# The experts' products taken in the order 0, 7, 1, 6, 2, 5, 3, 4, with one buffer and a share of the pooling moved beside it

## The chip, the core and the metric

One core of a Trainium2 chip runs the whole program in one launch. Its engines are TensorE (PE, with its weight loads listed as PEld), VectorE (DVE), ScalarE (ACT), GpSimd (POOL) and SyncE (SP), which issues most transfers; 16 DMA engines move the data. The metric is the time of one execution on the device in microseconds (us), the median of several runs.

## The reference, cut to what matters

Three layers follow one another: attention (a pooled one plus a local one), a mixture of experts, and a mixing layer over tokens and channels. There are 4 batches of 576 tokens, 512 channels (8 heads of 64), 8 experts with 1024 hidden units, and 1536 hidden channels in the mixing layer.

```python
# attention: q, k, v averaged over 4 tokens for the pooled part; a band of +-3 tokens for the local part
k_d = k.reshape(B, H, Sd, factor, D).mean(axis=3)
out = repeat(sm_attn(q_d, k_d, v_d), 4) + softmax(band(q @ k.T)) @ v
# mixture of experts: one expert a token, chosen in order of the tokens
for s in range(S):
    fresh_e = int(np.argmax(logits[b, s]))
    e = fresh_e if s == 0 or local_gate[b, s] < 0.5 else prev_e
    h = np.maximum(x[b, s] @ w1[e], 0.0)
    out[b, s] = p[e] * (h @ w2[e])
# mixing: the weights are float64, a token product and then a channel product
u = x + (np.maximum(xt @ w_tok1, 0.0) @ w_tok2).transpose(0, 2, 1)
return (u + np.maximum(u @ w_ch1, 0.0) @ w_ch2).astype(np.float32)
```

## The kernel before, in words

The program has three stages, each with its own hand-written scheduler (`Sched`). A stage's code only lists operations; `Sched.order` then gives every engine a fixed order of instructions, from costs written in the source, from the free buffers and from a due time (`stage`) that the code sets while it lists them. The order is fixed before the program runs, so an engine that waits at one instruction also holds up all that stand behind it. Transfers that SP issues are one such queue.

**Attention** (`Attn`) runs over the 4 batches. `pool_k` adds up four keys at a time: either one reduction on VectorE (64x768 to 64x192), or three additions on GpSimd; the table `KDVE` lists the pairs of batch and half that go to VectorE. `pool_v` does the same for the values of the batches 1 to 3, on GpSimd from a ring of buffers `raw` (`NRAW` of them), into which the values are loaded. The ring `vw` (`NVW` buffers of the same size) holds the values of the local attention. `p` is the softmax of the local part: VectorE sums it, GpSimd divides by the sum. `route` numbers the tokens of each expert.

Behind the last batch's products, the two experts with most tokens so far get a first block of 256 rows each (`Early`). Its weights come chunk by chunk into `raw`, and are split into a high and a low part, which lie in the attention's rings `kz` (high) and `vw` (low). Each product of two fp32 matrices is made of three matrix products of such parts.

**The experts** (`Moe`) run by rank, which is the order of the experts by tokens left. Rank r has room for `CAPS[r]` rows: 384, 376, 320, 288, 256, 256, 192 and 128. A rank's weights come in 8 chunks of 512 KB, issued by SP into a ring of 3 buffers (`raw`, tiles `raw_27xx`), then split by ScalarE (`wh`, a cast) and VectorE (`wl`, a difference) into rings of 4 (3, and the pair `l_wh`, `l_wl`). For each chunk, `mm1` makes 128 hidden units of all the rank's rows (12 products with as many columns as rows, at least 256), ScalarE and VectorE make the two parts of the ReLU (`h`), and `mm2` adds them into the output in PSUM (`y`, 4 banks; three products of 512 columns a tile of 128 rows). Rank 7 is an exception: its `mm1` reads the unsplit `raw` buffer (4 products), so that this buffer is free only after `mm1`, and only half a chunk is split. `gather` fetches the rows of the next rank. Filling the spare rows of the output with zeros (`zeros`) takes 8 transfers of 512 KB and some small ones.

Every second chunk from the ninth to the forty-ninth also lists one `convert`, 21 in all: it turns 512 columns of the mixing layer's float64 weights into two fp32 parts. That is a transfer of 512 KB (`cr`), three operations on VectorE (`cf`), a square on ScalarE (`cs`), two operations on GpSimd (`cs`, `cf`), a cast on ScalarE and a difference on VectorE (`wtl`, `c1l`, `c2l`).

**The mixing layer** (`Mix`) then gathers the tokens' rows from memory (`yd`) and runs its products.

Of the kernel before, what the change touches and what calls it, by code (L numbers as in the profile page):

```python
# [21 lines left out]
NE = 8  # L22
# [13 lines left out]
KF = FF // 128  # L36
# [183 lines left out]
class Sched:  # L220
# [80 lines left out]
    def i(self, e, m, after=(), **kw):  # L301
        outs = [kw[k] for k in ("out", "accum_out") if kw.get(k) is not None]
        ins = [v for k, v in kw.items() if k not in ("out", "accum_out") and isinstance(v, (bass.AP, View))]
        acc = [(region(a), True) for a in outs] + [(region(a), False) for a in ins]
        c = self.cost(e, m, outs[0], ins, kw)
        if self.cur is not None:
            o = self.ops[self.cur]
            assert o["e"] == e
            o["calls"].append((m, kw))
            o["d"] += c  # L310
        else:
            self.ops.append(dict(e=e, calls=[(m, kw)], d=c, pred={}, use=[], init=None, stage=self.stage + self.shift, moves=True))
        k = len(self.ops) - 1
        o = self.ops[k]
        for p in after:
            o["pred"].setdefault(p, 0)
        for a in outs + ins:
            if isinstance(a, View) and a.buf not in o["use"]:
                o["use"].append(a.buf)
                a.buf.users.append(k)  # L320
        self.note(k, acc)
        return k
# [211 lines left out]
class Attn:  # L534
# [108 lines left out]
    def pool_k(self, b, pr):  # L643
# [5 lines left out]
        for u in range(2):  # L649
            r = slice(64 * u, 64 * u + 64)  # L650
            kv = kz[r, u, :, 3:195].rearrange("p h (g r) -> p h g r", r=4)
            kd = s["kd"][r, :, 48 * pr:48 * pr + 48]
            if (b, u) in KDVE:
                i("dve", "tensor_reduce", out=kd, in_=kv, axis=AX.X, op=ALU.add)
# [266 lines left out]
    def run(self, early):  # L921
        S_ = self.S
        do = lambda name, b, *args: S_.late((name, b), getattr(self, name), b, *args)
        do("load_q", 0)
        self.load_consts()
        for b in range(B):
            t0 = STEP * 3 * b
            S_.stage = t0 - D_LEAD * STEP if b else D0
            if b:
                do("load_q", b)  # L930
            for pr in range(3):
                do("load_u", b, pr)
                do("pool_k", b, pr)
                if pr:
                    do("pool_v", b, pr - 1)
            for hp in range(HP):
                do("pool_q", b, hp)
                do("d1", b, hp)
                do("d2", b, hp)
            for pr in range(3):  # L940
                S_.stage = t0 + STEP * pr
                do("l1", b, pr)
                do("l2", b, pr)
                for n in ((0,), (1, 2), (3, 4))[pr]:
                    do("x1", b, n)
            S_.stage = t0 + 3 * STEP + R_LAG * STEP
            if b == B - 1:
                stage, S_.stage = S_.stage, t0 + E_LAG * STEP
                S_.late("take", self.early.take)
                S_.stage = stage  # L950
            elif b == B - 2:
                S_.stage = t0 + 3 * STEP + E_LAG * STEP
            do("route", b)
            if b == B - 3:
                self.early = early()
# [142 lines left out]
def convert(S_, src, n, hi, lo, after=(), cf="cf", cs="cs", queue="dma"):  # L1098

    i = S_.i  # L1100
    raw = S_.next("cr")
    if src.dtype == mybir.dt.int64:
        i(queue, "dma_start", after=after, out=raw[:, 0:2 * n], in_=src.bitcast(I32))
        rv = raw[:, 0:2 * n].rearrange("p (n t) -> p n t", t=2)
        low, high = rv[:, :, 0], rv[:, :, 1]
        f = S_.next(cf, I32)[:, 0:n]
        i("dve", "tensor_scalar", out=f, in0=high, scalar1=3, scalar2=0x3FFFFFF8, op0=ALU.logical_shift_left, op1=ALU.bitwise_and)
        i("dve", "scalar_tensor_tensor", out=f, in0=low, scalar=29, in1=f, op0=ALU.logical_shift_right, op1=ALU.bitwise_or)
        i("dve", "scalar_tensor_tensor", out=f, in0=high, scalar=-0x40000000, in1=f, op0=ALU.bitwise_and, op1=ALU.bitwise_or)
        sq = S_.next(cs, F32)[:, 0:n]  # L1110
        i("act", "activation", out=sq, in_=high.bitcast(F32), func=AF.Square)
        f = f.bitcast(F32)
        i("pool", "tensor_single_scalar", out=sq, in_=sq, scalar=FLOOR, op=ALU.is_ge)
        i("pool", "tensor_tensor", out=f, in0=f, in1=sq, op=ALU.mult)
    else:
        f = raw.bitcast(F32)[:, 0:n]
        i(queue, "dma_start", after=after, out=f, in_=src)
    i("act", "copy", out=hi, in_=f)
    i("dve", "tensor_tensor", out=lo, in0=f, in1=hi.bitcast(F32), op=ALU.subtract)
# [249 lines left out]
            self.late("loadw", self.n)  # L1369


class Moe(Experts):
    LO, CUT, QUEUE = "dve", 4, "dma"

# [52 lines left out]
    def run(self):  # L1427
        NW = KF * NE
        prev, done = None, []
        t0 = 0.0  # L1430
        for n in range(NW):
            r, fb = divmod(n, KF)
            self.S.stage = t0
            t0 += 4 * (12 * CAPS[r] / 2400 + TILES[r] * 0.65)
            if n >= NLEAD:
                self.loadw(n)
            if fb == 3 and r + 1 < NE:
                self.gather(r + 1)
            h = self.mm1(r, fb)
            if prev is not None:  # L1440
                self.mm2(*prev)
            prev = (r, fb, h)
            done.append(len(self.S.ops) - 1)
            if n == 24:
                self.S.stage = t0
                self.zeros()
            if n >= 8 and n % CONV == 0 and self.jobs:
                self.S.stage = t0 + 60
                convert(self.S, *self.jobs.pop(0), after=(done[n - 6],))
        self.mm2(*prev)  # L1450
        assert not self.jobs
        self.S.issue(self.S.order(busy=dict(pe=PE_LATE)))
# [264 lines left out]


WARM, WINDOW = 0.5, 3.4
NKZ, NVW, NRAW = 5, 4, 3  # L1720
VPE = (0,)
KDVE = ((0, 0), (0, 1), (1, 0), (2, 0), (3, 0))
STEP, D_LEAD, R_LAG = 12.0, 1.0, 1.5
SLACK = 0.02
PE_LATE = 2.0
# [30 lines left out]
```

## Time and profile before

| what | value |
|---|---|
| median of 3 runs | 818.68 us (816.3 to 821.28) |
| the profiled execution | 815.2 us, of which 813.4 us are the span of the trace |
| PE, DVE, ACT, POOL busy | 764.6, 464.5, 331.1, 231.5 us |
| granted TensorE clock, mean | 0.987 |
| attention and early block | 0 to 214.9 us |
| experts | 214.9 to 438.3 us |
| mixing layer | from 448.0 us |

Engines work side by side, so their busy times don't add up to the span. A busy time says how much of a stretch an engine worked; what a change is worth is read from what the waiting engine waits for. Times in rows are microseconds from the start of the trace. The lines 525 to 531 belong to the scheduler's helper, which issues nearly every operation, so rows are told apart by the names of their tiles.

### The profile page before, as it was taken

What the parts mean: (1) busy time and instruction counts of PE and PEld (TensorE: products, weight loads), DVE (VectorE), ACT (ScalarE), POOL (GpSimd) and SP (SyncE); (2) the same over time, 40 slices, a digit from 0 to 9 for tenths busy, and PEclk for the clock granted to TensorE, in tenths of its full rate; (3) what the DMA queues carried; (4) which work ended last, traced back from release to release, by engine and by line L of the source; (5) the groups of instructions that cost most, each with busy time, mean ns of one, the idle gap of its engine ahead of it and who ended that gap; (6) DMA issues with size and microseconds to landing.
All of it is one profiled execution on the core that took longest, in us unless ns stands there. A gap on an engine that the chain in (4) does not pass through costs nothing. (4 is left out here: it accounts for less than half of the span.)

```text
span 813.4 us, 13914 instructions
## 1 busy us (share of the span) xinstructions
PE 764.6 (94%) x5318; PEld 635.8 (78%) x5318; DVE 464.5 (57%) x1025; ACT 331.1 (41%) x722; POOL 231.5 (28%) x191
## 2 busy tenths in 40 slices
PE   7898987978999998999896999999999999999998
PEld 4566774857898887888795887888888888888897
DVE  6688989696557878899952767531441144111121
ACT  1775867534435454666552534311321132110110
POOL 4676414450624546436401165200000000000000
PEclk9899999999999999999999999999999999999999
DMA  9986324636699866878664233002001200010010
GB/s 253 245 231 211 119 99 122 184 129 196 212 299 302 274 223 198 278 225 274 215 200 149 69 100 113 27 27 72 13 1 27 72 14 0 1 52 0 1 52 27
DMA packets 36346, 107.90 MB, mean 133 GB/s; under 512 B 5003, under 2 KB 5643, under 8 KB 35895
## 3 DMA queue, kind: packets, MB, share of 16 engines
q1 hardware_dynamic: 32359, 95.15, 37.2%
q0 software_dynamic: 3200, 10.28, 4.2%
q10 hardware_dynamic: 720, 1.57, 0.5%
q8 instruction: 42, 0.69, 0.3%
q14 instruction: 25, 0.20, 0.1%
HBM read 87.32 MB, written 19.66 MB: 132 GB/s over the span
## 5 line engine op out<-in xcount | busy, mean ns | idle before, releaser
L531 DVE SCALAR_TENSOR_TENSOR x_h<-x_m,x_h 128x512 fp32r<-128x512 f32 (+1 forms) x60 | 38.2, 637 | 194.9 <-ACT x_h L531 194.9
L527 PE MATMUL x_y<-x_h,c2h 128*128 128x512 f32 (+1 forms) x480 | 136.2, 369 | 0.0
L531 ACT ACTIVATE x_h<-x_m 128x512 fp32r<-128x512 f32 (+1 forms) x60 | 33.3, 554 | 201.1 <-PE x_m L527 176.1
L527 PEld LDWEIGHTS x_y<-x_h,c2h 128*128 128x128 f32 x480 | 86.6, 189 | 14.3
L527 PE MATMUL x_y<-x_h,c2l 128*128 128x512 f32 (+1 forms) x240 | 88.3, 368 | 0.0
L527 PE MATMUL y<-wh,h 128*128 128x512 f32 (+2 forms) x205 | 74.8, 402 | 1.8 <-DVE yo L531 1.2
L531 DVE TENSOR_TENSOR wl<-raw,wh 128x1024 fp32r<-128x1024 f32 (+1 forms) x47 | 59.9, 1277 | 18.4 <-ACT wh L531 18.0
L531 ACT CAST wh<-raw 128x1024 fp32r<-128x1024 f32 (+1 forms) x47 | 47.1, 1004 | 21.6 <-PE y L527 15.2
L531 POOL TENSOR_SCALAR cs<-cs 128x512 f32<-128x512 f32 (+1 forms) x21 | 38.1, 1812 | 49.8 <-ACT cs L531 49.1
L527 PEld LDWEIGHTS x_y<-x_h,c2l 128*128 128x128 f32 x240 | 45.2, 189 | 7.6
L527 PEld LDWEIGHTS y<-wh,h 128*128 128x128 f32 (+2 forms) x205 | 38.2, 188 | 12.1 <-DVE yo L531 2.5
L531 POOL TENSOR_TENSOR cf<-cf,cs 128x512 f32<-128x512 f32 (+1 forms) x21 | 39.6, 1884 | 27.9 <-DVE cf L531 26.3
L527 PE MATMUL y<-wl,h 128*128 128x512 f32 (+3 forms) x112 | 44.3, 395 | 0.0
L531 DVE SCALAR_TENSOR_TENSOR h<-m,h 128x256 fp32r<-128x256 f32 (+3 forms) x88 | 29.5, 358 | 8.5 <-ACT h L531 8.4
L531 ACT ACTIVATE h<-m 128x256 fp32r<-128x256 f32 (+6 forms) x64 | 25.4, 397 | 17.9 <-PE m L527 16.5
L531 DVE SCALAR_TENSOR_TENSOR cf<-cr,cf 128x512 int32<-128x512 int32 (+1 forms) x42 | 31.0, 739 | 0.7
L527 PE MATMUL m<-l_xh,wh 128*128 128x256 f32 (+2 forms) x96 | 29.2, 304 | 0.9 <-DVE h L531 0.9
L1126 POOL DMA_INDIRECT xg<-xd,q_xi x19 | 20.0, 1055 | 33.5 <-PE t L529 22.9
L527 PE MATMUL m<-l_xh,wl 128*128 128x256 f32 (+2 forms) x96 | 29.0, 302 | 0.2 <-DVE wl L531 0.2
L527 PE MATMUL m<-l_xl,wh 128*128 128x256 f32 (+2 forms) x96 | 28.8, 300 | 0.0
L531 ACT COPY pt<-pc 32x384 f32<-32x384 f32 x48 | 24.4, 509 | 10.7 <-DVE pc L531 10.0
L527 PE MATMUL y<-l_wh,h 128*128 128x512 f32 (+2 forms) x75 | 27.2, 402 | 1.1 <-DVE h L531 1.0
(810 smaller groups left out, 2035.8 us busy)
## 6 DMA issues: line engine op xcount, KB each, us to landing
raw<-in_wx SPq DMA_DIRECT2D x80, 512.0 KB
cr<-in_c SPq DMA_DIRECT2D x16, 512.0 KB
vw<-in_vw SPq DMA_DIRECT2D x12, 512.0 KB
kz<-in_kw SPq DMA_DIRECT2D x24, 200.0 KB
xd<-xn SPq DMA_DIRECT2D x16, 256.0 KB
yd<-zero SPq DMA_DIRECT2D x8, 512.0 KB
yd<-yo SPq DMA_DIRECT2D x15, 256.0 KB
x_cr<-in_c SPq DMA_DIRECT2D x7, 512.0 KB
```

The lines of the kernel that those rows point to most:

```text
L527: f(kw.pop("out"), **kw)
L531: f(**kw)
L1126: nc.gpsimd.indirect_dma_start(out=t.real()[0:n, :], out_offset=None, in_=table, in_offset=bass.IndirectOffsetOnAxis(ap=index, axis=0))
```

## The change

The loop over chunks takes the ranks in the order of a table, `TURNS`, in place of 0 to 7: the turn `n // 8` looks up its rank, and the rows of the next turn's rank are gathered four chunks ahead. The due times follow the turns. The converts stay with the same chunk numbers, so they now stand beside the ranks 7, 1, 6, 2 and 5, and one beside rank 3. In the attention, `vw` has 5 buffers in place of 4, `raw` 2 in place of 3, and of the key pooling only batch 0 stays on VectorE.

```diff
+TURNS = [0, 7, 1, 6, 2, 5, 3, 4]
...
-            r, fb = divmod(n, KF)
+            turn, fb = divmod(n, KF)
+            r = TURNS[turn]
             self.S.stage = t0
             t0 += 4 * (12 * CAPS[r] / 2400 + TILES[r] * 0.65)
             if n >= NLEAD:
-                self.loadw(n)
-            if fb == 3 and r + 1 < NE:
-                self.gather(r + 1)
+                self.loadw(KF * r + fb)
+            if fb == 3 and turn + 1 < NE:
+                self.gather(TURNS[turn + 1])
...
-NKZ, NVW, NRAW = 5, 4, 3
+NKZ, NVW, NRAW = 5, 5, 2
 VPE = (0,)
-KDVE = ((0, 0), (0, 1), (1, 0), (2, 0), (3, 0))
+KDVE = ((0, 0), (0, 1))
```

GpSimd in the attention, between the softmax of batch 0's first third and that of its second (`p_124`), before: `kd` are pooled keys, `vd` pooled values, `kz` the loaded keys.

```order
L531 TENSOR_TENSOR kd_116<-kz_89 64x4x48
L531 TENSOR_TENSOR kd_116<-kd_116,kz_89 64x4x48
L531 TENSOR_TENSOR kd_116<-kz_90 64x4x48
...
L531 TENSOR_TENSOR vd_117<-raw_105 72x512
L531 TENSOR_TENSOR vd_117<-raw_106 72x512
L531 TENSOR_TENSOR kd_116<-kz_86 64x4x48
L531 TENSOR_TENSOR kd_116<-kd_116,kz_86 64x4x48
L531 TENSOR_TENSOR vd_117<-vd_117,raw_107 72x512
...
L531 TENSOR_TENSOR kd_115<-kz_87 64x4x48
L531 TENSOR_TENSOR p_124<-p_124,sm_135 128x512
```

The same place now:

```order
L531 TENSOR_TENSOR kd_116<-kz_89 64x4x48 x2
L531 TENSOR_TENSOR kd_116<-kz_90 64x4x48 x2
L531 TENSOR_TENSOR kd_116<-kd_116,kz_89 64x4x48 x2
...
L531 TENSOR_TENSOR vd_117<-raw_106 72x512
L531 TENSOR_TENSOR kd_116<-kz_86 64x4x48 x2
L531 TENSOR_TENSOR kd_116<-kd_116,kz_86 64x4x48 x4
L531 TENSOR_TENSOR p_124<-p_124,sm_135 128x512
```

All 18 additions of batch 1's keys now stand ahead of that softmax, where 10 stood, and one addition of values, where 5 stood.

SP's queue in the experts' stage, from the tenth chunk's load on, before (`zero` fills spare rows of the output, `cr` is a convert's load, `yo` an output tile of rank 0); the chunks from the eighth load on are rank 1's:

```order
L1157 DMA raw_2717<-in_wx 128x1024
L531 DMA yd<-zero 128x2x512
...
L1157 DMA raw_2718<-in_wx 128x1024
L531 DMA cr_2705<-in_wt 128x1024
L531 DMA yd<-zero 128x2x512
...
L1157 DMA raw_2719<-in_wx 128x1024
L531 DMA yd<-zero 128x2x512 x2
```

The same place now; here the chunks from the eighth load on are rank 7's:

```order
L1157 DMA raw_2720<-in_wx 128x1024
L531 DMA yd<-zero 128x2x512 x3
L531 DMA cr_2708<-in_wt 128x1024
L531 DMA yd<-zero 128x2x512
...
L1157 DMA raw_2721<-in_wx 128x1024
...
L1157 DMA raw_2722<-in_wx 128x1024
L531 DMA yd<-zero 128x2x512
L531 DMA yd<-yo_2714 128x512
```

Five transfers of 512 KB stand between the tenth and the eleventh load, where one stood.

VectorE as rank 0 ends, now (`wl` of 512 columns are rank 7's, `h` of 128 its ReLU, `l_xl` rows of rank 6; the `wl` of 1024 is rank 1's first):

```order
L531 SCALAR_TENSOR_TENSOR h_2718<-m_2738,h_2718 128x128
L531 TENSOR_TENSOR wtl<-cf_2710,wth 128x512
L531 TENSOR_TENSOR l_wl_197<-raw_2722,l_wh_196 128x512
L531 SCALAR_TENSOR_TENSOR h_2719<-m_2738,h_2719 128x128
...
L531 TENSOR_TENSOR l_xl<-t_2736,l_xh 128x4x128
...
L531 TENSOR_TENSOR wl_2726<-raw_2720,wh_2723 128x1024
L531 TENSOR_TENSOR wl_2727<-raw_2721,wh_2724 128x512
```

Rank 7's chunks stand here, with rank 1's first chunk ahead of rank 7's last three.

## Rows read from the trace of the kernel before

**Rows 1.** Windows: busy time (instructions) of PE, PEld, DVE, ACT, POOL; clock, DMA share, GB/s.
```profile
0.00:90.00 90.00, 76.15 (x1107) 54.25 (x1108) 67.92 (x159) 55.08 (x184) 56.69 (x67) 0.96 0.83 229
90.00:143.90 53.90, 45.93 (x699) 34.04 (x697) 47.94 (x190) 39.49 (x114) 14.57 (x17) 0.97 0.33 105
143.90:214.90 71.00, 62.87 (x441) 53.86 (x442) 49.97 (x163) 28.92 (x53) 26.03 (x18) 0.98 0.56 179
214.90:289.50 74.60, 73.95 (x384) 65.48 (x383) 51.77 (x69) 37.51 (x57) 32.31 (x21) 1.00 0.82 268
289.50:401.80 112.30, 106.60 (x628) 91.40 (x627) 97.67 (x149) 66.81 (x108) 55.71 (x33) 0.98 0.74 241
401.80:438.30 36.50, 34.55 (x222) 30.01 (x222) 21.17 (x45) 16.81 (x34) 2.14 (x1) 1.00 0.65 209
438.30:448.00 9.70, 3.65 (x19) 2.17 (x17) 0.49 (x1) 1.12 (x2) 3.13 (x4) 0.82 0.26 81
448.00:813.40 365.40, 360.95 (x1826) 304.62 (x1826) 127.54 (x255) 85.42 (x174) 40.95 (x33) 1.00 0.11 37
```
**Rows 2.** Instructions on the tile kd: duration in ns (least, median, most), first and last start.
```profile
L531 POOL TENSOR_TENSOR kd<-kd,kz x18: 679/692/705, 24.3 to 87.7; 64x192 f32<-64x192 f32 x18
L531 DVE TENSOR_REDUCE kd<-kz x15: 903/935/952, 9.4 to 87.6; 64x192 f32<-64x768 f32 x15
L531 POOL TENSOR_TENSOR kd<-kz x9: 692/693/708, 23.6 to 86.2; 64x192 f32<-64x192 f32 x9
```
**Rows 3.** Waits of PE, 0 to 215 us: total us, times, longest.
```profile
PE m L527 <- DVE r_ev L531: 3.9, 1, 3.9
```
**Rows 4.** Timeline of the early block: a chunk's load issued, and its cast.
```profile
172.29 0.35 SPq L1157 DMA_DIRECT2D raw<-in_wx  x1
...
176.35 1.06 ACT L531 CAST kz4x<-raw 128x1024 fp32r<-128x1024 f32 x1 [0.99 <-DMA raw<-in_wx]
```
**Rows 5.** Timeline of PE: start, length, instruction; the first of a run of products each.
```profile
225.25 0.39 PE L527 MATMUL y<-wh,h 128*128 128x512 f32 x1
...
227.31 0.33 PE L527 MATMUL m<-l_xh,wh 128*128 128x384 f32 x1
...
229.42 0.39 PE L527 MATMUL y<-wh,h 128*128 128x512 f32 x1
...
368.45 0.28 PE L527 MATMUL m<-l_xh,wh 128*128 128x256 f32 x1
...
369.89 0.40 PE L527 MATMUL y<-wh,h 128*128 128x512 f32 x1
...
422.79 1.61 PE L527 MATMUL m<-xg,raw 128*128 128x128 f32 x13
```
**Rows 6.** Windows of 4 us in rank 0, columns as in rows 1.
```profile
228.00:232.00 4.00, 4.00 (x21) 3.63 (x21) 2.61 (x3) 1.74 (x3) 0.00 (x0) 1.00 1.01 383
...
236.00:240.00 4.00, 4.00 (x22) 3.63 (x22) 2.14 (x3) 1.95 (x3) 1.40 (x1) 1.00 0.94 339
240.00:244.00 4.00, 4.00 (x22) 3.63 (x22) 2.74 (x4) 1.12 (x2) 2.50 (x2) 1.00 0.69 159
244.00:248.00 4.00, 4.00 (x24) 3.75 (x22) 3.09 (x6) 2.82 (x5) 1.68 (x1) 1.00 1.03 333
```
**Rows 7.** Timeline of SP: the tenth chunk's load issued.
```profile
240.56 0.34 SPq L1157 DMA_DIRECT2D raw<-in_wx  x1
```
**Rows 8.** Groups of DVE, 215 to 440 us: count, busy us, mean ns, idle before.
```profile
L531 DVE TENSOR_TENSOR wl<-raw,wh 128x1024 fp32r<-128x1024 f32 x42 | 56.5, 1346 | 13.0 <-ACT wh L531 12.6
L531 DVE SCALAR_TENSOR_TENSOR cf<-cr,cf 128x512 int32<-128x512 int32 x40 | 29.6, 741 | 0.7
```
**Rows 9.** Instructions on the tile raw: duration in ns (least, median, most), first and last start.
```profile
L531 DVE TENSOR_TENSOR wl<-raw,wh x47: 691/1219/2325, 219.8 to 435.4; 128x1024 fp32r<-128x1024 f32 x42, 128x512 fp32r<-128x512 f32 x5
```
**Rows 10.** Timeline near 273 us: a convert on POOL, a weight split on DVE.
```profile
273.03 1.32 POOL L531 TENSOR_TENSOR cf<-cf,cs 128x512 f32<-128x512 f32 x1 [0.84 <-DVE cf L531]
...
273.11 2.32 DVE L531 TENSOR_TENSOR l_wl<-raw,l_wh 128x1024 fp32r<-128x1024 f32 x1
```

## The prediction

> **What bounds the kernel now.** I read the windows by stage first, to see which engine is full where, then PE's waits in each stage, then the timeline at the places that the change touches. From 448.0 us on, in the mixing layer, PE is busy 360.95 of 365.4 us and DVE 127.54 [rows 1]: nothing that the change touches works there, and the layer starts when the last expert's rows are written. So the mixing layer counts for nothing (at most 0.5 us to either side, from a hand-over of 9.7 us whose last rank now has two output tiles in place of one). What is left is 438.3 us: attention with the early block to 214.9, and the experts.
>
> In the experts PE is also the fullest, but not alone. From 289.5 to 401.8 (from the first ReLU of rank 2 to the last of rank 5, where converts run) DVE is busy 97.67 of 112.3 us; from 214.9 to 289.5 the DMA engines are busy 82% of the time; from 401.8 on (ranks 6 and 7) DVE is down to 21.17 of 36.5 us and POOL to 2.14 [rows 1]. So three resources take turns, and a change of order moves the stretches in which each is short.
>
> **PE's own work.** From one run of products to the next, 9 products of 512 columns take 2.06 us (0.229 each), 12 of 384 take 2.11 (0.176), 12 of 256 take 1.44 (0.120), and 13 unsplit ones of 128 take 1.61, the last of them 0.28, so 0.111 each [rows 5]. Between 256 and 384 columns I go on a straight line. A chunk then needs: rank 0, 2.11 + 2.06 = 4.17 us; rank 1, 4.13; rank 2, 3.61; rank 3, 3.44; ranks 4 and 5, 2.81; rank 6, 2.59; rank 7, 1.13. A rank is 8 chunks: 33.4, 33.0, 28.9, 27.5, 22.5, 22.5, 20.7, 9.0. With 16 gathered tiles of four transposes (0.45 us each, an estimate from the products of 128 columns) that is 204.7 us, where the stage took 223.4: 18.7 us are lost to waits and to filling the pipeline after them. The order of ranks changes none of the 204.7, only the 18.7.
>
> **Rank 7 early.** A chunk of rank 7 keeps PE for 1.13 us and needs 512 KB. In full slices of 4 us the DMA engines moved 333 to 383 GB/s [rows 6], so such a transfer takes about 1.5 us: rank 7 can't run at PE's pace without loads ahead of it, and only three buffers lie ahead, each held until its mm1. At the end of the stage, before, it cost the last 36.5 us [rows 1] about 5 us: PE's sum there is 20.7 + 9.0 + 1.4 + 0.45 = 31.6. Now it comes second. SP issued the tenth load at 240.56 [rows 7], and that load waits for the same as now. Behind it now stand three fills, a convert's load and a fourth fill, 5 transfers or 7.6 us, on a queue that had caught up (159 GB/s from 240 to 244 [rows 6]). So the eleventh load lands at about 252 by the queue; by its buffer, which is free when rank 7's first mm1 is through at about 250.5, plus about 4 us (a load issued at 172.29 let its cast start at 176.35 [rows 4]), at 254.5. I take the later one. Then, at 1.5 us each: the twelfth at 256, a fill, three half-size output tiles, and the loads thirteen to seventeen with one convert's load, the last at 268.5. Cast, difference and mm1 of that chunk, the second of rank 1, add 4.5: its ReLU at 273. PE's own sum to there is 33.4 + 9.0 + 4.1 + 2.1 + 8 tiles of 0.45 - 0.7 = 51.5, so 266.4, and with the 2.4 us that rank 0 lost before, 268.8. The stall is 4.2 us, about the 5 that vanish at the end. From both sides: 0, if loads keep ahead, and 11, if the transfers run at the stage's mean of 268 GB/s [rows 1], 1.96 us each, which puts the seventeenth 7 us later.
>
> **The stretch with converts.** Before, from 289.5 to 401.8, PE's sum is 104.4 us (four ranks, 9 tiles) and DVE's busy time 97.67 [rows 1]; the stretch took 7.9 more than the one and 14.6 more than the other. Now it goes from that ReLU at 273 to the last of rank 5: seven mm2 and six mm1 of rank 1, ranks 6, 2 and 5, one mm1 of rank 3, 6 tiles: 102.5 us of PE. On DVE 31 weight splits (1.346 us in the mean), 49 convert passes (0.741 for two in three) and smaller ones stand there [rows 8]; by the same means the stretch before adds up to 104.8 where DVE was busy 97.67 (neighbours overlap), so 110.4 counts as 102.9. By PE's excess it takes 110.4 us, by DVE's 117.5; I take the middle, 114. That DVE has as much to do as PE is the price of the new order: the converts sit beside 114 us of PE work in place of 134, while ranks 3 and 4, at the end, have none. After it stand 1.4, rank 3's other 25.9, rank 4's 22.5, 0.9 and 1.5 of waits: 52 us. The stage ends at 273 + 114 + 52 = 439, before 438.3. The sum of the experts is 0.7 us later; bounds 8 us earlier (268.8 + 110.4 + 51) and 13 later (280 + 118 + 53).
>
> The row of a weight split that takes 2.32 us shows a convert's operation on POOL that began 0.08 us before it and ran 1.32 [rows 10], and the median of all is 1.219 [rows 9]. The Trainium skill ("SBUF — State Buffer", section "Who interferes with whom") says why: a VectorE instruction with two inputs in SBUF and a GpSimd one that reads SBUF exclude each other for a whole instruction, and the later one blocks. The trace agrees, 1.32 us of POOL lengthening DVE by 1.1. By that rule the new order, with more converts and splits to the microsecond, meets more such pairs; it is the rival below that ends slower.
>
> **The attention.** Nine reductions of 0.935 us leave DVE, 8.4 us; 27 additions of 0.69 us come to POOL, 18.7 us [rows 2]. POOL was busy 56.69 of the first 90 us, DVE 67.92, and from 90 to 143.9 DVE 47.94 [rows 1]. So POOL has room for them (75.4 of 90), if they don't hold up its softmax; in the place shown, eight additions of keys more (5.5 us) stand ahead of the second softmax, and four of values fewer, each over 512 elements a row in place of 192, so it should be as early. What the early block's start waits for is batch 2's routing on DVE, and there PE has its longest wait of the stage, 3.9 us [rows 3]. Of the 8.4 us I count 3 as gained, somewhat below that wait, since much of DVE's relief falls where it was idle a quarter of the time. Bounds: 8.4 gained, and 5 lost, if POOL's queue is what is late (seven additions of keys, 4.8 us, ahead of one softmax).
>
> The fifth vw buffer and the third raw buffer gone: a raw buffer's turn is 4.06 us to the cast, 1.06 of cast and 1.22 of difference [rows 4, 9], 6.3 in all, so two buffers give a chunk each 3.2 us. The early block's 16 chunks took 71 us, 4.4 each, PE's own part 2.8. So it costs nothing at that pace; if everything else were gone, 0.4 us a chunk, 6 us, which I leave to the range.
>
> **Sum.** Attention -3.0, experts +0.7 - and I round this to 0, the working being no finer - mixing 0: 3 us less. The profiled execution took 815.2, the median is 818.7, 3.5 above; on the median that is 815.7.
>
> **Rivals.** First, the loads keep ahead: rank 7 passes without a stall between rank 0's and rank 1's long chunks, and the stretch with converts runs at PE's excess. For it: the queue had caught up at 240 us [rows 6], and rank 1's first chunk now stands among rank 7's last, so PE has work while it waits. Against it: three buffers. The experts end 8 us earlier: 818.7 - 8 - 3 = 807.7. Second, DVE decides (slower): from rank 1's end to rank 5's DVE stays full, 117.5 us, and five more pairs of split and convert meet at 1.1 us: 123, so 273 + 123 + 52 = 448, 9.7 later; less 3, about 825.5. It decides from the point at which DVE's busy share of that stretch passes 95%. For it: DVE was at 87% of that stretch [rows 1] with 94 us of work to 100 of PE's, and now has 100 to 100; against it, rank 1, the longest of the ranks with converts, comes before the short ones and can take converts early. Third, POOL's queue in the attention is late and takes 5 us: with the experts even, 823.5. Fourth, the relief on DVE is not on the path at all, and the time stays at 818.7.
>
> **How the numbers follow.** The forecast, 815.7, has 0.45, with its own range 811 to 821; the first rival 0.24, the second 0.18, the third 0.08, the fourth 0.05. Half a per cent, about what a measurement of this kernel can tell from none, is 4.1 us: 814.6 to 822.8. Of the forecast's 0.45, 0.18 lie below that, 0.25 inside, 0.02 above. Faster: 0.18 + 0.24 = 0.42. Slower: 0.02 + 0.16 + 0.04 = 0.22. The rest, 0.36, is no change. The range from 805 to 827 takes in the first two rivals.
>
> **What the changed profile would show.** PE waiting near 255 us, for a raw load, 3 to 6 us in all; a last rank that runs at 2.8 us a chunk; DVE's busy share from 273 to 387 near 90%; the first product of the experts at about 212 us. I am wrong if rank 7's chunks pass at under 1.4 us, if the experts' stage differs from 223.4 us by more than 5, or if the experts begin later than 215 us.

## The result, and the profile after

The change makes the kernel slower: 830.43 us in the median of 9 runs against 818.68, ratio 1.0139 [1.0111, 1.0168]; 815.7 was predicted. (Ratios leave out runs more than 1.5% above the fastest of their kernel; of e2 below, the kernel with the attention alone, three of six runs are left, so its ratio and its median differ, and the traces of e2 and e14 are of runs left out.) The profiled execution of after is one of its longer ones (834.43 us, of which 832.6 are the span), that of before one of its shorter ones (815.2). So the two traces differ by 19.2 us where the medians differ by 11.8, and what is read from the two side by side is somewhat too large.

The windows of after, with the columns of [rows 1]. The first four rows split the attention and the early block at the first product on batch 2's `r_dg` (the routing), at the start of `e_xi` (the rows that the routing gives to the early block), and at the early block's first product; then come the experts in three parts, the hand-over and the mixing layer.

```profile
0.00:135.20 135.20, 112.62 (x1716) 82.44 (x1716) 99.70 (x294) 87.05 (x285) 83.01 (x104) 0.97 0.68 184
135.20:157.30 22.10, 17.46 (x142) 13.41 (x141) 18.63 (x55) 11.44 (x24) 10.04 (x9) 0.61 0.30 92
157.30:169.30 12.00, 6.87 (x58) 5.47 (x55) 8.65 (x26) 4.01 (x9) 6.35 (x5) 0.87 0.74 203
169.30:231.80 62.50, 54.21 (x321) 46.37 (x319) 41.76 (x130) 20.51 (x33) 11.93 (x8) 0.92 0.41 131
231.80:294.30 62.50, 58.30 (x321) 51.02 (x321) 39.04 (x60) 30.87 (x54) 27.64 (x21) 0.98 0.94 334
294.30:404.00 109.70, 105.68 (x604) 91.66 (x604) 102.38 (x153) 68.78 (x110) 64.82 (x36) 0.99 0.77 251
404.00:456.40 52.40, 52.22 (x312) 45.08 (x310) 30.08 (x48) 24.49 (x37) 1.30 (x1) 1.00 0.47 143
456.40:466.10 9.70, 3.70 (x18) 2.39 (x17) 1.18 (x2) 0.52 (x1) 3.17 (x4) 0.67 0.33 107
466.10:832.60 366.50, 362.46 (x1826) 306.01 (x1826) 127.44 (x255) 85.38 (x174) 40.72 (x33) 0.99 0.11 37
```

The experts begin at 231.8 us, 16.9 later than in [rows 1]; their stage takes 224.6 us (223.4 before), hand-over and mixing 376.2 (375.1). So 16.9 of the 19.2 us lie ahead of the experts. The trace of before, cut at the same four events:

```profile
0.00:124.90 124.90, 108.45 (x1630) 79.78 (x1631) 98.63 (x293) 81.44 (x269) 62.92 (x76) 0.97 0.69 195
124.90:139.65 14.75, 10.70 (x135) 6.22 (x135) 13.63 (x49) 9.71 (x23) 4.72 (x4) 0.90 0.35 114
139.65:151.90 12.25, 10.92 (x138) 8.95 (x138) 8.19 (x20) 9.03 (x17) 9.10 (x9) 0.98 0.53 157
151.90:214.90 63.00, 54.87 (x347) 47.20 (x346) 45.38 (x150) 23.31 (x41) 20.55 (x13) 0.97 0.55 176
```

The routing's product comes 10.3 us later, and PE runs 86 more instructions ahead of it (4.2 us more of busy time; the rest is idle); from there to `e_xi` it takes another 7.4 us longer, at a granted clock of 0.61; the third stretch is as long as before but has 6.87 us of PE's work in place of 10.92. Part of the work that filled PE in that stretch is already done. In PE's order all of batch 3's three local scores (`sl`) stand ahead of the routing's product; before, two of them did. The last of them in after:

```profile
132.36 0.39 PE L527 MATMUL sl<-maskb,identb 128*128 128x512 bf16 x1
132.68 1.04 PE L527 MATMUL sl<-kz,qt 128*24 128x60 f32 x64
133.65 0.85 PE L529 MATMUL g<-ca,pd 128*72 128x128 f32 x6
135.18 0.27 PE L527 MATMUL g<-r_dg,utri 128*128 128x256 f16 x1 [0.68 <-POOL r_dg L531]
```

The pooled keys of after (columns as in [rows 2]), and PE's longest waits before 232 us, which answer to [rows 3]:

```profile
L531 POOL TENSOR_TENSOR kd<-kd,kz x36: 673/684/1370, 28.0 to 96.3; 64x192 f32<-64x192 f32 x36
L531 POOL TENSOR_TENSOR kd<-kz x18: 685/692/708, 24.7 to 91.8; 64x192 f32<-64x192 f32 x18
L531 DVE TENSOR_REDUCE kd<-kz x6: 935/948/952, 11.5 to 18.7; 64x192 f32<-64x768 f32 x6
```

```profile
PE sl L527 <- DVE pd1x L531: 7.0, 3, 5.6
PE sl L527 <- DMA kz<-in_kw: 4.2, 1, 4.2
...
PE m L527 <- DVE r_ev L531: 0.8, 1, 0.8
```

The first of these waits lies in the early block (the 5.6 us end at 194.1), whose stretch is no longer than before: 62.5 us against 63.0. The nine reductions have become 27 additions at the price foreseen. The wait of 3.9 us for `r_ev` has shrunk to 0.8, as hoped, but the time was not gained.

### The profile page after: what moved, and what is told of

Read it like the earlier page. It is cut to its first block, busy times and chain, and to the rows that moved or that the text cites. A ratio compares the mean times of both kernels' runs of the same rounds, so it can differ in the third digit from the quotient of the medians.

```text
span 832.6 us, 13922 instructions
## 1 busy us (share of the span) xinstructions
PE 773.5 (93%) x5302; PEld 643.9 (77%) x5302; DVE 468.9 (56%) x1016; ACT 333.0 (40%) x722; POOL 249.0 (30%) x218
## 3 DMA queue, kind: packets, MB, share of 16 engines
q1 hardware_dynamic: 32359, 95.15, 36.5%
## 5 line engine op out<-in xcount | busy, mean ns | idle before, releaser
L527 PEld LDWEIGHTS y<-wh,h 128*128 128x128 f32 (+2 forms) x215 | 40.1, 186 | 8.6 <-DVE h L531 0.4
L531 POOL TENSOR_TENSOR cf<-cf,cs 128x512 f32<-128x512 f32 (+1 forms) x21 | 37.0, 1761 | 27.1 <-DVE cf L531 25.9
L531 DVE SCALAR_TENSOR_TENSOR cf<-cr,cf 128x512 int32<-128x512 int32 (+1 forms) x42 | 34.0, 813 | 0.5
L531 DVE SCALAR_TENSOR_TENSOR h<-m,h 128x256 fp32r<-128x256 f32 (+4 forms) x88 | 29.3, 356 | 7.6 <-ACT h L531 7.5
L527 PE MATMUL pv<-pt,vw 128*64 128x96 f32 x384 | 24.1, 273 | 9.1 <-ACT pt L531 3.4
L1126 POOL DMA_INDIRECT xg<-xd,q_xi x19 | 21.9, 1153 | 29.1 <-DVE pd1x L531 17.9
L527 PEld LDWEIGHTS pv<-pt,vw 128*64 128x64 f32 x384 | 19.0, 151 | 14.8 <-DVE xt L531 5.0
L527 PE MATMUL m<-l_xh,wl 128*128 128x256 f32 (+1 forms) x96 | 28.9, 301 | 1.4 <-DVE wl L531 1.4
L527 PE MATMUL m<-l_xh,wh 128*128 128x256 f32 (+1 forms) x96 | 28.7, 299 | 0.0
```

Source lines behind the costliest of these rows:

```text
L527: f(kw.pop("out"), **kw)
L531: f(**kw)
L1126: nc.gpsimd.indirect_dma_start(out=t.real()[0:n, :], out_offset=None, in_=table, in_offset=bass.IndirectOffsetOnAxis(ap=index, axis=0))
```

## The experiments

The table lists the sixteen runs: median, ratio to before on the same chip with its interval, and from each run's trace the starts of the routing's product, of `e_xi` and of the experts' first product, in us. A trace is one execution; the ratio decides.

| run | median | ratio | product | e_xi | experts |
|---|---|---|---|---|---|
| before | 818.68 | | 124.9 | 139.7 | 214.9 |
| after | 830.43 | 1.0139 [1.0111, 1.0168] | 135.2 | 157.3 | 231.8 |
| e1 turns only | 818.13 | 0.9965 [0.9939, 0.9992] | 122.7 | 137.4 | 211.3 |
| e2 attention only | 835.38 | 1.0112 [1.0044, 1.0181] | 136.7 | 158.5 | 231.9 |
| e3 key pooling only | 829.32 | 1.0106 [1.0075, 1.0138] | 132.4 | 147.3 | 226.3 |
| e4 buffers only | 823.59 | 1.0030 [0.9992, 1.0068] | 130.0 | 147.9 | 219.3 |
| e5 old order, additions | 825.06 | 1.0079 [1.0052, 1.0105] | 133.9 | 148.6 | 222.1 |
| e6 new order, old work | 829.82 | 1.0142 [1.0101, 1.0184] | 134.6 | 149.5 | 228.7 |
| e7 after, more filler | 829.94 | 1.0136 [1.0091, 1.0181] | 137.6 | 158.5 | 232.4 |
| e8 turns, rank 7 last | 818.83 | 0.9996 [0.9966, 1.0027] | 126.2 | 140.9 | 214.1 |
| e9 after, 3 scores held | 819.81 | 1.0032 [0.9996, 1.0068] | 125.9 | 141.3 | 216.2 |
| e10 after, 2 held | 829.59 | 1.0151 [1.0102, 1.0199] | 127.6 | 150.4 | 221.5 |
| e11 turns, 3 held | 816.62 | 0.9987 [0.9958, 1.0015] | 125.5 | 138.0 | 214.3 |
| e12 turns, 2 held | 821.73 | 1.0054 [1.0018, 1.0090] | 127.8 | 142.9 | 222.6 |
| e13 after, late splits | 829.31 | 1.0130 [1.0086, 1.0173] | 133.9 | 150.3 | 225.5 |
| e14 e9, late splits | 824.81 | 1.0065 [1.0035, 1.0095] | 130.4 | 142.4 | 223.8 |
| e15 e1, late splits | 819.30 | 1.0004 [0.9967, 1.0042] | 126.8 | 139.4 | 220.2 |
| e16 e11, late splits | 817.25 | 0.9972 [0.9946, 0.9999] | 123.8 | 137.6 | 212.4 |

**Which part costs.** The four parts apart. e1, against after:

```diff
-NKZ, NVW, NRAW = 5, 5, 2
+NKZ, NVW, NRAW = 5, 4, 3
-KDVE = ((0, 0), (0, 1))
+KDVE = ((0, 0), (0, 1), (1, 0), (2, 0), (3, 0))
```

> The new order of ranks with the attention of before (4 and 3 buffers, five pairs of key pooling on VectorE). Theory A (the loss is all ahead of the experts: between the first products and the early block's first rows; the turns themselves are even): 819.5 us, within 1.5 of before, the experts' stage 223 to 226 us where before had 223.4 and the kernel after 224.6. Rival B (the turns cost as much as the attention, since rank 7 early starves PE and the converts press on VectorE): 824 or more, with a stage of 229. Rival C (the turns gain what the attention hides): 814 or less, a stage of 219.

e2 is before with both lines of after:

> The ranks in the order 0 to 7, with the attention of after (5 and 2 buffers, two pairs on VectorE). Theory A: about 829.5 us, 11 above before, with the experts' first product near 230 us instead of 214.9 and their stage unchanged at 223. Rival B: 824, and the rest is found in the turns. Rival C: 834, the attention losing more than the whole change does.

e3 is before with the line `KDVE` of after, e4 before with `NKZ, NVW, NRAW = 5, 5, 2`:

> Before with nothing but the key pooling moved (two pairs on VectorE, 27 additions more on GpSimd). If GpSimd's queue is the cause (theory A1: additions ahead of the local softmaxes, so batch 2's routing is late and the early block waits for its rows): 827 or more, with batch 2's routing (the start of its r_dg) near 132 us, where before had 123.2 and after 134.5. If the buffers are the cause (rival A2): 819 or less, the routing at 123.

> Before with nothing but the buffers changed (5 value buffers, 2 raw buffers). If two raw buffers or the earlier fifth load are the cause (theory A2: the values' pooling of batches 2 and 3 was 23 to 28 us later in the trace of after): 826 or more, batch 2's routing near 132 us. If GpSimd's queue is (theory A1): 819 within 1.5, routing at 123. If the two only hurt together (rival A3): both this one and the one with the key pooling moved stay below 822.

Theory A holds in the times: the turns alone lose nothing (the ratio says 0.35% gained, some 2.9 us), and the attention alone loses 1.12%, most of what the whole change loses. Its figures for the experts' stage don't: 228.8 us in e1 and 226.7 in e2, where 223 to 226 and 223 were expected. Within the attention the key pooling is the larger part (1.06%, with the routing's product 7.5 us later than in before, as theory A1 has it). For the buffers 0.30% is not clear of none, though the product comes 5.1 us later, between what A1 and A2 said. After and e2, with the same attention, begin the experts at 231.8 and 231.9.

**Work or order.** Moving the pooling changes the work of two engines, and with it the order that the scheduler writes for all of them. e5 and e6 cross the two: an operation is placed as one thing and issued as another, as the entry `swap` says (the comments on e5 and e6 are not in the kernels). e5 is before with this edit, e6 is e3 with it.

```diff
+                k = i("dve", "tensor_reduce", out=kd, in_=kv, axis=AX.X, op=ALU.add)
+                if b:  # e5: placed as a reduction, issued as three additions
+                    self.S.ops[k]["swap"] = [("tensor_tensor", dict(out=kd, ...), "pool") for n in range(1, 4)]
...
+                    if u == 0:  # e6: placed as three additions, issued as one reduction
+                        self.S.ops[o]["swap"] = [("tensor_reduce", dict(out=kd, ...), "dve")] if k == 3 else []
```

> Every engine's order is that of before; only where VectorE's seven reductions for the batches 1 to 3 that the table moves stood in that order, GpSimd now gets three additions each. Theory L (load: the additions on GpSimd are what delays batch 2's routing, by standing ahead of softmaxes and by blocking VectorE's small instructions): 827 us or more, as with the table moved and a new order (829.3). Theory P (plan: the work can go to GpSimd at no cost, and the loss comes from the order that the scheduler writes for it, with batch 3's scores ahead of batch 2's last products): 817 to 821, batch 2's routing (first r_dg) near 123 us.

(The reductions are nine, not seven.)

> The other cross: the order that the scheduler writes with the key pooling moved (as in the run with only that table changed, 829.3 us), but half of the sums that would be on GpSimd, those of the first 64 rows, are issued as reductions on VectorE where the third addition would stand. Theory P: 826 or more, since the order is what costs. Theory L: 821 or less, since GpSimd has its old load or less back.

Both cost. With the division of work of before, the order that comes with the moved pooling loses 1.42%, as much as after: here theory P's number comes. In the order of before, the additions lose 0.79%: less than theory L wanted, and more than theory P allowed (817 to 821 us, the routing near 123; it came at 133.9). Neither number is a share: together they are 2.2%, and e3, which has both, loses 1.06%. In each run the issued operations also stand where the scheduler didn't plan them, and that can cost by itself; no run takes it apart. GpSimd in e5, up to the second and third softmax of batch 0 (`p`):

```profile
39.22 1.26 POOL L531 TENSOR_TENSOR vd<-vd,raw 72x512 f32<-72x512 f32 x1
40.57 0.68 POOL L531 TENSOR_TENSOR kd<-kd,kz 64x192 f32<-64x192 f32 x1
41.32 1.26 POOL L531 TENSOR_TENSOR vd<-vd,raw 72x512 f32<-72x512 f32 x1
42.55 0.69 POOL L531 TENSOR_TENSOR kd<-kz 64x192 f32<-64x192 f32 x1
43.31 1.43 POOL L531 TENSOR_TENSOR kd<-kd,kz 64x192 f32<-64x192 f32 x2
44.81 1.45 POOL L531 TENSOR_TENSOR kd<-kz 64x192 f32<-64x192 f32 x2
46.34 1.43 POOL L531 TENSOR_TENSOR kd<-kd,kz 64x192 f32<-64x192 f32 x2
47.73 2.04 POOL L531 TENSOR_TENSOR p<-p,sm 128x512 f32<-128x512 f32 x2
```

and the same softmaxes before:

```profile
39.45 2.05 POOL L531 TENSOR_TENSOR p<-p,sm 128x512 f32<-128x512 f32 x2 [0.45 <-DVE sm L531]
```

They come 8.3 us late, behind a queue without a gap, and PE then waits 6.7 us in one place for `xt`, for which its longest wait in before was 0.9:

```profile
PE pv L527 <- DVE xt L531: 6.7, 1, 6.7
```

In the new order those softmaxes come at 40.2 in e3, with 0.5 us idle ahead of them:

```profile
40.17 2.05 POOL L531 TENSOR_TENSOR p<-p,sm 128x512 f32<-128x512 f32 x2 [0.49 <-DVE sm L531]
```

So there the scheduler has put the additions elsewhere. (With the buffers moved too they come at 40.1 in e2 and, behind a queue without a gap, at 42.2 in after.)

**The clock and the ranks.** e7 is after with `WARM = 0.8` in place of 0.5; e8 is e1 with another table:

```diff
-TURNS = [0, 7, 1, 6, 2, 5, 3, 4]
+TURNS = [0, 1, 6, 2, 5, 3, 4, 7]
```

> The changed kernel with one number changed, WARM 0.8 in place of 0.5, which fills more of the idle places that the plan sees on TensorE in the attention with small products that nothing uses. Theory C (part of the loss is the clock: the runs of after had a mean granted clock of 0.973 in the median, those of before 0.981): clock back to 0.98 and 825 us or less. Rival: the idle places on the chip aren't those of the plan, so the clock and the 830 us stay within 2; or the extra products stand ahead of needed ones, and it is 832 or more.

> The attention of before, the ranks in the order 0, 1, 6, 2, 5, 3, 4, 7: rank 7 stays last, the rest is as in the new order. Theory E (the prediction's: rank 7 costs about as much early, in loads that come late, as it does last): within 2 of the run with only the new order of ranks (818.1). Rival 1 (rank 7 early is where the 0.35% come from): 821 or more. Rival 2 (rank 7 early costs, and pairing long and short ranks is what gains): 815 or less.

In e7 the mean granted clock came back to 0.9805 (median of its runs; 0.973 in after, 0.981 in before), and the time stayed: theory C falls. In its trace the stretch from the routing's product to `e_xi` has a clock of 0.76 in place of 0.61 and takes 20.9 us in place of 22.1, but the product comes 2.4 us later than in after. Whether the added products delay it is not shown. In e8 rank 7 costs as much last as it does early, within what the runs can tell: theory E.

**The order held.** e9 makes batch 3's scores wait for the routing's products (`gate` is set in `route`, at the last product on `r_dg`); e10 does the same with `pr >= 1`, and e11 and e12 are the two edits on e1.

```diff
-        with self.group("pe"):
+        with self.group("pe", after=(self.gate,) if b == 3 and pr >= 0 else ()):
...
+        self.gate = len(self.S.ops) - 1
```

> The changed kernel, with all three of batch 3's local scores made to wait for the products of batch 2's routing, so that the scheduler can't place them ahead (in the order of after all three stand ahead, in that of before two). Theory F (what the new order costs is that batch 3's work, which covers the wait for batch 2's routing, is used up ahead of it: in after that product came at 135.2 us, before at 124.9): the routing's product at 128 or earlier, the experts at 225 or earlier where after had 231.8, and 823 us or less. Rival G (batch 3 is then late itself, and the last routing holds up the experts): the routing earlier, but the experts not before 229, and 828 or more.

> As the run before, but only the second and third of batch 3's local scores wait. Theory F: between the two, some 824 to 828 us, the routing's product near 131. Rival G: 829 or more.

> The kernel with only the order of ranks changed (818.1 us, attention as before), and batch 3's three local scores made to wait for batch 2's routing. Theory F: two scores stood ahead of it before, so there is a little to gain: 814 to 818. Rival G: batch 3's own products end later, 820 or more.

> As the run before, with only the second and third of batch 3's local scores waiting, so that one stands ahead in place of two. Theory F: 815 to 818. Rival G: 819 or more.

e9 does the same work with the same buffers as after and takes 819.81 us: 10.6 of the 11.8 us are back. That total has in it what the turns may gain. Against e11, which has the same gate and the attention of before and ran on the same chip, e9 is 3.2 us longer in the median (3.8 in the mean, give or take 2.6), so with the gate the attention of after still costs something. Its windows, cut at the four events:

```profile
0.00:125.90 125.90, 104.68 (x1485) 77.51 (x1485) 94.89 (x286) 81.62 (x269) 81.04 (x102) 0.96 0.72 194
125.90:141.30 15.40, 12.05 (x243) 9.17 (x247) 12.08 (x40) 7.61 (x19) 5.75 (x5) 0.89 0.31 96
141.30:151.60 10.30, 7.58 (x115) 5.00 (x102) 6.82 (x16) 6.90 (x14) 9.38 (x11) 1.00 0.37 103
151.60:216.20 64.60, 58.69 (x412) 49.62 (x410) 48.20 (x159) 26.61 (x48) 15.84 (x11) 1.00 0.54 167
```

PE has 1485 instructions ahead of the routing where after had 1716, and the clock stays at 0.89 or more. But the step between fails: with two scores held (e10) nothing is gained, and with the attention of before (e12) the time is 0.54% above before. Theory F foresaw gains in both. So the number of scores ahead of the routing is not the measure; each edit rewrites the whole order. e10's profiled execution was its shortest (822.07), so its trace doesn't show where the others lose. e11 is within what theory F foresaw, but not told from e1.

**The blocked instructions.** From the routing's product to `e_xi` after took 22.1 us. There weight splits of the early block run on GpSimd:

```profile
136.01 2.35 POOL L531 TENSOR_TENSOR vw2x<-raw,kz2x 128x1024 fp32r<-128x1024 f32 x1
138.31 2.35 POOL L531 TENSOR_TENSOR vw3x<-raw,kz3x 128x1024 fp32r<-128x1024 f32 x1
...
148.37 2.34 POOL L531 TENSOR_TENSOR vw4x<-raw,kz4x 128x1024 fp32r<-128x1024 f32 x1
```

and beside them, on VectorE, one instruction of 2.21 us and five of 4.20 together:

```profile
138.47 2.21 DVE L531 TENSOR_TENSOR r_W<-r_W,r_W 128x5 f32<-128x5 f32 x1
...
147.13 4.20 DVE L531 TENSOR_SCALAR r_ev<-ca,r_eh 128x144 f16<-128x144 f32 x5
```

The same instructions of the same routing before:

```profile
126.44 0.17 DVE L531 TENSOR_TENSOR r_W<-r_W,r_W 128x5 f32<-128x5 f32 x1
...
135.38 1.38 DVE L531 TENSOR_SCALAR r_ev<-ca,r_eh 128x144 f16<-128x144 f32 x5
```

e13 to e16 make these splits wait for `e_xi`:

```diff
-        self.S.i(lo, "tensor_tensor", out=wl[:, c], ...)
+        self.S.i(lo, "tensor_tensor", after=self.taken if lo == "pool" else (), out=wl[:, c], ...)
...
+        self.taken = (len(S_.ops) - 1,)
```

> The changed kernel, with the early block's weight splits on GpSimd made to wait until batch 2's routing has given its rows (e_xi). In the trace of after three of them (2.35 us each) stand in that stretch, and single small instructions of the routing on VectorE take 0.7, 2.2 and 2.8 us longer beside them. Theory K (these blocked instructions carry the chain, and so a good part of the loss): 826 or less, the stretch from the routing's product to e_xi 17 us or less where after had 22.1. Rival F (the loss is the order of batch 3's work; the blocked instructions stood in before's chain as well, 1.0 and 2.3 us): 828 or more.

> The run in which batch 3's three scores wait (819.8 us), with the splits on GpSimd waiting too. Theory K: 3 us and more below it, 817 or less. Rival H (with two raw buffers the later splits hold up the early block's loads): 821 or more.

> The new order of ranks with the attention of before (818.1 us), with the splits on GpSimd waiting for e_xi. Theory K: 815 to 817, since two instructions of the chain were 3 us longer in the trace of before. Rival H: 819 or more.

> The new order of ranks, the attention of before, batch 3's scores waiting for the routing's products (816.6 us), and the splits on GpSimd waiting for e_xi. Theory K: 813 to 815. Rival H: 817 or more.

In e13 the stretch shrinks from 22.1 to 16.4 us, as theory K has it:

```profile
133.90:150.30 16.40, 12.96 (x123) 10.01 (x123) 12.86 (x51) 7.33 (x16) 2.38 (x4) 0.79 0.05 17
```

Of the 5.7 us, 4.1 are the two blocked places (0.17 and 2.17 us in e13); the clock, 0.79 in place of 0.61, changed as well. The median is 829.31 against 830.43: the 826 or less of theory K doesn't come, though a gain of 3 or 4 us is not ruled out by six runs (the means differ by 1.1, give or take 3.6). e13's trace begins the experts 6.3 us earlier than after's, but that trace is 4.0 us longer than after's median. In e9, too, the instruction on `r_W` took 2.26 us (the five on `r_ev` 1.42), and of the 15.6 us by which its trace begins the experts earlier than after's, 9.3 are there ahead of this stretch. So this blocking is not the main thing that tells e9 from after. The late splits cost in e14, 5 us above e9; rival H puts that down to the two raw buffers, which no run shows. e15 and e16 are not told from e1 and e11, and theory K's numbers for them don't come. The routing's product of e13 still comes at 133.9.

e1 and e16 are the two that beat before, by 0.35% and 0.28%; the intervals of both end just below one. Those of e8, e11 and e15, also with the attention's work of before and a new order of ranks, include one. Among sixteen runs two such intervals are little to go by: that the turns gain is not shown.

## Why the prediction was wrong, point by point

**The attention, -3.0 us: the step that failed.** The prediction had 3 us gained there and at most 5 lost. It cost 1.12% (e2), some 9 us, or 12.3 by the medians of after and e1; with it the time passed the top of the range, 827. The step took the order as given, looked at GpSimd's queue in one place, and concluded that a softmax "should be as early". At that place it nearly is (40.2 in e3, 42.2 in after, 39.5 before). But the scheduler had written another order for all engines, and the order decides more than the instructions that changed engine: e6 has the division of work of before and loses 1.42%; e9 has the work and the buffers of after and is 10.6 us faster than it. The two orders showed it before any run: three of batch 3's scores ahead of batch 2's routing, where two had stood. I didn't look there, although I had named that routing as what the early block waits for.

The wait for that routing, 3.9 us, from which the 3 us gained were taken, did shrink to 0.8, but in after the routing itself came 10.3 us later, and the experts began at 231.8 us, past the 215 that the prediction had named as a sign of being wrong. GpSimd's queue, the third rival, is seen at its full size in the old order alone (e5, 8.3 us); that it costs less in the new one is likely, not shown. VectorE's relief doesn't show in its busy time: 168.74 us up to the experts, against 165.83 before, with 8.4 us of reductions gone, so other instructions took 11 us more; GpSimd was busy 111.3 in place of 97.3 (sums of the four rows). The rule of the Trainium skill that the prediction cited ("SBUF — State Buffer", section "Who interferes with whom") is borne out by the 2.21 us above, for a single small instruction with two inputs as well; in e13 freeing such instructions gained nothing that the runs can tell.

**The buffers, nothing (up to 6).** 0.30% [-0.08, 0.68], some 2.5 us: inside the bounds.

**The experts, +0.7 us.** The trace has +1.2 (224.6 against 223.4), and e1's ratio says -0.35%, about -2.9 us [-5.0, -0.7]. The sum held, in part by luck: two terms of it were off by 4 us each, in opposite ways. To the ReLU of rank 1's second chunk 58.1 us were predicted and 62.5 measured; the stretch with converts was to take 114 and took 109.7; the rest 52, and took 52.4. In the first, PE's own sum was too small: the 4 products that the source lists for a chunk of rank 7 run as 8 instructions, 64 in its 8 chunks, in before's trace too (the 13 in [rows 5] are part of a longer run):

```profile
L527 PE MATMUL m<-xg,raw x64: 270/275/377, 266.4 to 287.9; 128*128 128x128 f32 x64
```

By the prediction's 0.111 each that is 1.58 us a chunk in place of 1.13, 3.6 us more for the rank. So in before the end of the stage had lost 1.3 us, not 5 (36.5 less 35.2), and rank 7 early had little to win back. The time to that ReLU was 7.4 us above PE's sum, which is 55.1 with the 8; the prediction had 6.6 above its 51.5. The stall was there, smaller and later than thought: 0.85 us for a load, and 2.0 for the splits of rank 1's second chunk, whose cast had itself waited for its load. From 291 to 295, behind that wait, the granted clock was 0.68 in the mean. The rows of these waits:

```profile
280.34 1.16 PE L527 MATMUL m<-xg,raw 128*128 128x128 f32 x8 [0.85 <-DMA raw<-in_wx]
...
289.12 1.04 ACT L531 CAST wh<-raw 128x1024 fp32r<-128x1024 f32 x1 [1.61 <-DMA raw<-in_wx]
290.21 0.45 PE L527 MATMUL m<-xh,wh 128*128 128x376 f32 x1 [1.39 <-ACT wh L531]
291.47 0.44 PE L527 MATMUL m<-xh,wl 128*128 128x376 f32 x1 [0.65 <-DVE wl L531]
```

In the stretch with converts the prediction took the middle between PE's way (110.4) and VectorE's (117.5): PE's was right, with 109.7. VectorE was busy 102.38 of it, 93%, under the 95% from which the second rival decides. A weight split took 1.221 us in the median, as in [rows 9]:

```profile
L531 DVE TENSOR_TENSOR wl<-raw,wh x48: 683/1221/2316, 237.7 to 449.2; 128x1024 fp32r<-128x1024 f32 x43, 128x512 fp32r<-128x512 f32 x5
```

The last rank ran at 2.8 us a chunk, as foreseen.

**The mixing layer, nothing.** Hand-over and mixing took 1.1 us more in the trace of after; in the eighteen traces the layer, from its first `x_t` to the end, takes 364.7 to 366.8 us (366.5 in after, 365.4 in before), so this is not told from chance.

**What stays open.** Which place of the new order costs the time is not settled. What goes with it in all eighteen traces is the routing's product: the nine executions that had it at 122.7 to 127.8 took 813.5 to 822.1 us, the nine that had it at 130.0 to 137.6 took 825.1 to 836.6. That is a sign and not a cause shown: e5 has it late (133.9) in the old order, e13 has a shorter stretch behind it and the same time, and e10's median (829.59) is far above its traced execution.

## What to carry to other kernels

Where a scheduler writes the order, an edit of one operation's engine is an edit of every engine's order: compare the orders around the longest chain first (here a routing that the next block waits for), and count what now stands ahead of it. Work that could cover a wait may be used up ahead of it; e9 gained by keeping it, e10 and e12 did not. To tell work from order, place an operation as before and issue it as after, and the reverse: two runs show whether each can cost. They don't give shares (here 1.42 and 0.79%, and 1.06 for both), and a cross that issues an operation where it wasn't planned may have a cost of its own.

## What was not expected of the hardware

- A VectorE instruction that took 0.17 us in before took 2.21 in after, beside a GpSimd split of 2.35 us, and five that took 1.38 together took 4.20. I had thought of the exclusion for large pairs only.
- In after the granted clock was 0.50, the lower of its two levels (1.2 GHz of 2.4), from 139 to 155 us; PE had been busy 0.91 us of the two from 135 to 137, and 1.64 of the next two. With more products in the idle places the median over runs of the mean clock rose from 0.973 to 0.9805, and the time stayed.
- The experts' stage with the new order of ranks took 222.4 to 228.8 us in the traces of ten runs (after, e1, e7, e9 to e13, e15 and e16), and with the old one 223.4 to 228.7 in those of before and e3 to e6. A single trace doesn't show a gain of 3 us in it.
